# The first three tiles' attention in float32 as loaded, and the next three tiles' scores too

## The chip, the cores and the metric

The kernel runs on one core of a Trainium2 chip. The core has a matrix engine (TensorE, PE in the rows, with its weight loads as PEld), a vector engine (VectorE, DVE), an activation engine (ScalarE, ACT), a general engine (GpSimd, POOL) and a queue that issues transfers (SyncE, SP). The metric is the device time in microseconds (us) of one execution, as a median over runs. One further execution was recorded by the hardware profiler; all rows below come from it.

## The reference

The input is q, k and v of 4 batches, 8 heads, 768 positions and a head size of 64, weights of two further layers, and two integers.

```
scores = scale * q @ k.T + bias          # bias: -slope[h] * distance
scores = where(global or local, scores, -1e9)   # first 8 columns; 96 columns back
a = softmax(scores);  x = a @ v                 # x: 3072 x 512
h = x @ w_in;  x2 = (h * sigmoid(h)) @ w_out    # 512 -> 2048 -> 512
# then a soft mixture of experts: 32 slots, softmax of x2 @ phi
# over tokens and over slots, 8 small two-layer experts, and back
```

All of it is float32 in the reference; w_in and w_out arrive as float64.

## The kernel before

The 3072 rows are 24 tiles of 128. Six tiles make a batch (t is the tile's number in its batch, u its slot in a ring of four for keys and values). A tile attends to its own 128 columns and, unless t is 0, to the tile before it, whose first eight columns are overwritten with the batch's global columns (kg for keys, vg for values). Chunks of three tiles go through the two dense layers: `l1_step` makes 128 hidden columns of a chunk, `l2_part` the second layer.

Precision comes from float16 pairs. `hi` (lines 191 to 195) rounds a value to float16, `lo` (199 and 201) makes the float16 remainder, and a product is three TensorE matmuls. HE, HLO, PHE, PLE are strings that name for each tile the engine of these steps (A is ACT, V is DVE, P is POOL). `split(T)` does this for q, k and v of a tile, `s_step(T, pr)` computes the scores of two heads (line 293), the bias and maximum (298, DVE) and the exponential (299, ACT), and after each second pair splits four heads' probabilities and turns them with a transfer that transposes (314). `flip` is the other way to turn: TensorE transposes in float32 (214) into a PSUM bank, from which `hi` and `lo` read. PTE names for the first three tiles which half uses it; before, only the last of six does. `pv_step(T, half)` multiplies the turned probabilities by v (336), and for half 1 normalises (344 to 346) and makes the transposed float16 pair of the result that `l1_step` reads.

The first six tiles (`paired`) have q and k of two heads stacked on 128 partitions, so that a head's score matmul uses 64 partitions; the others have the layout of q_l and k_l. Loads go to the staging buffers stage_m, for tiles 1 and 2 to space that is used later.

`conv(p)` turns one of 16 pieces of float64 weights (1 MB each, loaded by `w_ahead` at 411 into a ring of places) into float16 pairs, with steps on DVE (421, 429, 430, 448), ACT (428, 440, 443) and POOL (426, 446). Pieces 0 to 7 are w_in and 8 to 15 w_out. GATE holds some loads back until a given half tile of probabilities is done.

`first_items` gives the order of the first three tiles. The other tiles' steps (`other_items`) are spread over the dense steps of the chunk before them: tiles 3 to 5 are done while chunk 0 goes through the dense layers. On each engine the instructions then stand in a fixed order, and an engine works through its own in that order; the transfers of the SP queue likewise.

## Time and profile before

| what | us |
|---|---|
| median of 3 runs | 766.43 |
| lowest and highest | 765.55 and 767.75 |
| the profiled execution | 765.0 |
| its span, first to last instruction | 763.2 |

The span is what the rows cover; 1.8 us of the execution lie around it. Busy time of an engine is the time in which it had an instruction under way. The rows of one engine can be read against a window of the span. [...]

### The profile page before, as it was taken

Reading aid. Unit: us, or ns where it says so; the run is one execution under the profiler, and the core shown is the slowest. Engines: PE = TensorE matmul, PEld = TensorE weight load, DVE = VectorE, ACT = ScalarE, POOL = GpSimd, SP = SyncE. Lnnn points to the kernel's source line nnn. Section 1 sums busy time; section 2 is a strip of 40 time slices with the busy share of each in tenths; the row PEclk is TensorE's granted clock in tenths of the full one; section 3 lists DMA queues with packets and bytes.
Section 4 is the critical chain, followed back from the end, with each engine's and each line's share of the span. In section 5 each row is a group of like instructions: output and inputs, shape, how many; then the busy total and the mean of one; then the engine's idle time right before and its main releaser. Section 6 shows DMA issues by size and latency. Waiting matters only on the chain.

```text
span 763.2 us, 14337 instructions
## 1 busy us (share of the span) xinstructions
PE 683.0 (89%) x5559; PEld 395.0 (52%) x5559; DVE 489.0 (64%) x1108; ACT 336.6 (44%) x855; POOL 324.7 (43%) x267
## 2 busy tenths in 40 slices
PE   2477757598999999999999999999999999998995
PEld 1244423244655565556556654665466546665375
DVE  6999999997775487548735873597266306505232
ACT  7756786553552255245423542454156305303122
POOL 4689684733455356415633673337324320101000
PEclk9978969799999999999999999999999999999997
DMA  6787645565456355733563567354532694295987
GB/s 237 194 249 205 218 87 152 191 181 120 75 125 139 83 113 137 174 75 77 132 138 74 107 137 167 56 111 109 86 43 43 150 320 178 97 357 214 391 330 223
DMA packets 162747, 120.22 MB, mean 158 GB/s; under 512 B 137456, under 2 KB 147184, under 8 KB 156656
## 3 DMA queue, kind: packets, MB, share of 16 engines
q1 hardware_dynamic: 162672, 119.23, 58.4%
q8 instruction: 45, 0.74, 0.4%
q14 instruction: 30, 0.25, 0.1%
HBM read 79.10 MB, written 6.29 MB: 112 GB/s over the span
## 4 chain that ended last, share of the span: by engine, by line
PE 67%; DVE 16%; issue 5%; POOL 4%; DMA 4%; ACT 3%; SPq 0%; ACTq 0%; DVEq 0%; POOLq 0%
PE bank L480 8%; PE bank L481 8%; PE bank L482 8%; PE bank L460 8%; PE bank L462 8%; PE bank L461 8%; PE bank L293 4%; PE bank L336 3%; DVE arena L201 2%; DMA arena<-arena 2%; DVE arena L199 2%; POOL arena L193 2%; PE bank L864 2%; DVE arena L429 2%; PE bank L902 2%
## 5 line engine op out<-in xcount | busy, mean ns | idle before, releaser
L193 POOL TENSOR_SCALAR arena<-arena 128x1024 f16<-128x1024 f32 (+5 forms) x146 | 144.4, 1002 | 237.0 <-ACT arena L299 102.5
L460 PE MATMUL bank<-rows,arena 128*128 128x384 f16 x512 | 168.4, 330 | 6.2 <-ACT arena L191 4.0
L462 PE MATMUL bank<-rows,arena 128*128 128x384 f16 x512 | 168.3, 329 | 0.8 <-DVE arena L448 0.8
L461 PE MATMUL bank<-rows,arena 128*128 128x384 f16 x512 | 168.3, 329 | 0.0
L191 ACT ACTIVATE arena<-bank 128x384 f16<-128x384 f32 (+2 forms) x165 | 81.8, 505 | 177.0 <-DVE bank L466 98.7
L199 POOL TENSOR_TENSOR arena<-arena 128x1024 f16<-128x1024 f32 (+2 forms) x69 | 131.0, 1900 | 41.3 <-ACT arena L191 37.3
L299 ACT ACTIVATE arena<-arena 128x256 f32<-128x256 f32 (+1 forms) x192 | 92.2, 482 | 98.2 <-DVE arena L298 95.3
L481 PE MATMUL bank<-arena 128*128 128x512 f16 x336 | 128.9, 384 | 2.7 <-POOL arena L446 1.9
L480 PE MATMUL bank<-arena 128*128 128x512 f16 x336 | 129.1, 384 | 1.5 <-DVE arena L201 1.5
L482 PE MATMUL bank<-arena 128*128 128x512 f16 x336 | 128.7, 383 | 0.0
L201 DVE SCALAR_TENSOR_TENSOR arena<-bank,arena 128x384 f16<-128x384 f32 (+2 forms) x142 | 81.3, 572 | 32.7 <-ACT arena L191 32.0
L293 PE MATMUL bank<-arena 128*128 128x256 f16 (+3 forms) x432 | 63.4, 288 | 41.5 <-DVE arena L298 23.9
L298 DVE CUSTOM_DVE_ANT_0 arena<-bank,arena 128x256 f32<-128x256 f32 (+1 forms) x192 | 70.5, 395 | 44.2 <-PE bank L293 42.8
L466 DVE SCALAR_TENSOR_TENSOR bank<-arena,bank 128x384 f32<-128x384 f32 x128 | 71.2, 557 | 31.0 <-ACT arena L464 29.8
L199 DVE TENSOR_TENSOR arena<-arena 128x1024 f16<-128x1024 f32 (+2 forms) x50 | 74.7, 1496 | 12.6 <-POOL arena L193 12.2
L464 ACT ACTIVATE arena<-bank 128x384 f32<-128x384 f32 x128 | 61.9, 484 | 21.1 <-PE bank L462 20.8
L293 PEld LDWEIGHTS <-arena 128*128 128x128 f16 (+1 forms) x432 | 36.3, 101 | 66.5 <-issue 38.1
L462 PEld LDWEIGHTS <-arena 128*128 128x128 f16 x512 | 50.4, 99 | 35.4 <-issue 1.6
L461 PEld LDWEIGHTS <-arena 128*128 128x128 f16 x512 | 50.4, 98 | 34.5 <-issue 7.2
L460 PEld LDWEIGHTS <-arena 128*128 128x128 f16 x512 | 50.5, 99 | 31.4 <-issue 2.9
L482 PEld LDWEIGHTS <-arena 128*128 128x128 f16 x336 | 33.1, 99 | 43.9 <-issue 5.3
L480 PEld LDWEIGHTS <-arena 128*128 128x128 f16 x336 | 33.2, 99 | 38.1 <-issue 4.8
(174 smaller groups left out, 808.8 us busy)
## 6 DMA issues: line engine op xcount, KB each, us to landing
arena<-in_w_dram SPq DMA_DIRECT2D x31, 1024.0 KB, 7.4
arena<-in_q_l_dram SPq DMA_DIRECT2D x18, 512.0 KB, 3.7
arena<-in_k_l_dram SPq DMA_DIRECT2D x18, 512.0 KB, 4.0
arena<-in_w_in_dram SPq DMA_DIRECT2D x8, 1024.0 KB, 5.7
arena<-in_w_out_dram SPq DMA_DIRECT2D x8, 1024.0 KB, 4.9
arena<-in_v_l_dram SPq DMA_DIRECT2D x24, 256.0 KB, 3.0
out_dram<-arena SPq DMA_DIRECT2D x4, 768.0 KB, 7.6
out_dram<-arena SPq DMA_DIRECT2D x8, 384.0 KB, 5.0
```

What stands on the lines that cost most here:

```text
L191: A.activation(out=out, in_=in_, func=AF.Copy, scale=p2(e))
L193: G.tensor_scalar(out=out, in0=in_, scalar1=p2(e), scalar2=0.0, op0=ALU.mult, op1=ALU.add)
L199: (V if eng == "V" else G).tensor_tensor(out=out, in0=in_, in1=h, op=ALU.subtract)
L201: V.scalar_tensor_tensor(out=out, in0=in_, scalar=p2(e), in1=h, op0=ALU.mult, op1=ALU.subtract)
L293: mm(sp[i][:, :w] if t == 0 else sp[i].rearrange("p (s c) -> p s c", s=2), qd[r, 4 * y + h], kv, start=(j == 0), stop=(j == len(terms) - 1))
L299: A.activation(out=pw, in_=pw, func=AF.Exp, scale=-1.0, bias=nmx[:, T, h:h + 1], accum_out=psum_[T % 2][:, h:h + 1])
L460: mm(hp, wh, x[:, 0, k], start=(k == 0), stop=False)
L461: mm(hp, wh, x[:, 1, k], start=False, stop=False)
L462: mm(hp, wl, x[:, 0, k], start=False, stop=(k == 3))
L480: mm(op, gh, woh[:, f, 0], start=(f == 0), stop=False)
L481: mm(op, gh, woh[:, f, 1], start=False, stop=False)
L482: mm(op, gl, woh[:, f, 0], start=False, stop=(f == 15))
```

## The change

Tiles 0 to 2 keep q, k and v as the float32 numbers that were loaded. Their scores are one float32 matmul per head (before: three of float16), their probabilities are turned on TensorE in float32 and copied by ACT to float32, and the product with v is one float32 matmul per head and block (before: three). No float16 parts of q, k or the probabilities are made for them, and of v only those of tile 2 and of the eight global rows, which tile 3 needs. Tiles 3 to 5 have float32 scores too, from q and k as loaded; their probabilities and v stay in pairs.

The float32 keys lie in the same ring as the pairs did (kr32 is a view of kr: z is now the half of a tile's columns), so a tile's keys are loaded by two transfers with runs of 64 numbers. q of these tiles goes to q16's buffers and to a part of stage_m, v to other parts of it. The global rows of v reach tile 1's buffer by a small transfer from memory, in place of a POOL copy. The load of tile 5 stands after tile 3's last score step, before it stood ahead of the third; that of tile 4 stays behind the split of tile 3. The scale of v, which the pairs carried, goes into the normalisation.

```
--- before.py
+++ after.py
@@ -89,7 +89,7 @@
 BE = 'A'
 NPAIR = 6
 HLO = 'VPVVVV'
-PTE = 'DDDDDA'
+PTE = 'A'
 XTE = 'VDA'
 GLE = 'PQPVPPVPPVPPPPVP'
 GATE = {1: (0, 0), 2: (0, 1), 3: (1, 0), 4: (1, 1), 5: (2, 0), 6: (2, 1)}
@@ -180,6 +180,14 @@
         p16 = [ar.new([2, 4, 256], F16) for _ in range(2)]
         pt0 = ar.off
         pt = [ar.new([2, 4, 2, 128], F16) for _ in range(2)]
+
+        kr32 = kr.bitcast(F32)
+        kg32 = kg.rearrange("p z h c -> p (z h c)").bitcast(F32)[:, 0:32].rearrange("p (h c) -> p h c", h=H // 2)
+        q32 = [q16[i].rearrange("p h c -> p (h c)").bitcast(F32).rearrange("p (h c) -> p h c", h=H // 2) for i in range(2)]
+        q32.append(stage_m[0][:, 0:4])
+        v32 = [stage_m[2].rearrange("p (h d) -> p h d", h=H)] + [stage_m[1][:, 4 * i:4 * i + 4].rearrange("p a c -> p (a c)").rearrange("p (h d) -> p h d", h=H) for i in range(2)]
+        v_next = stage_m[0][:, 4:8].rearrange("p a c -> p (a c)")
+        pt32 = [ar.view(pt0 + 4096 * i, [1024], F32) for i in range(2)]
         psum_ = [ar.new([H], F32) for _ in range(2)]
         rinv = [ar.new([H], F32) for _ in range(2)]
         x1f = ar.new([H, D], F32)
@@ -237,35 +245,47 @@
 
             return T < NPAIR
 
+        def q_of(T):
+            return q32[2 if T == 2 else T % 2]
+
         def load(T, bufs):
             if paired(T):
-                bufs = [bufs[0][:, 0:4], bufs[1][:, 0:4], bufs[2]]
-            for s, src in zip(bufs, (q_f, k_f, v_l) if paired(T) else (q_l, k_l, v_l)):
+                nc.sync.dma_start(out=q_of(T), in_=q_f[T])
+                for z in range(2):
+                    nc.sync.dma_start(out=kr32[:, z, 0:4, T % NR], in_=k_f[T][:, :, 64 * z:64 * z + 64])
+                nc.sync.dma_start(out=v32[T].rearrange("p h d -> p (h d)") if T < C0 else v_next, in_=v_l[T])
+                return
+            for s, src in zip(bufs, (q_l, k_l, v_l)):
                 nc.sync.dma_start(out=s, in_=src[T])
             staged[T] = bufs
 
         def split(T):
-            qs, ks, vs = staged.pop(T)
             t, u = T % TPB, T % NR
             he = HE[T] if T < len(HE) else "P"
             le = HLO[T] if T < len(HLO) else "V"
-            qd = q16[T % 2]
-            n = 4 if paired(T) else 8
             if paired(T):
-                qh, ql, qf = qd[:, 0:4], qd[:, 4:8], qs
+                v3 = v32[T] if T < C0 else v_next.rearrange("p (h d) -> p h d", h=H)
+                if T == 0:
+                    hi("P", kg32, kr32[:, 0, 0:4, u, 0:8], 0)
+                    hi("A", vg[0:8, :, 0], v3[0:8], E_V)
+                    lo("V", vg[0:8, :, 1], v3[0:8], E_V, vg[0:8, :, 0])
+                elif T >= C0 - 1:
+                    hi(he, v16[:, u, :, 0], v3, E_V)
+                    lo("V", v16[:, u, :, 1], v3, E_V, v16[:, u, :, 0])
+                if T == C0 - 1:
+                    hi("P", v16[0:8, u], vg[0:8], 0)
             else:
-                qh, ql, qf = qd, qd[64:128], qs[64:128]
-            hi(he, qh, qs, E_QK)
-            lo("P" if le == "P" else "V", ql, qf, E_QK, qh if paired(T) else ql)
-            hi(he, kr[:, 0, 0:n, u], ks, E_QK)
-            lo("V" if le == "V" else "P", kr[:, 1, 0:n, u], ks, E_QK, kr[:, 0, 0:n, u])
-            v3 = vs.rearrange("p (h d) -> p h d", h=H)
-            hi(he, v16[:, u, :, 0], v3, E_V)
-            lo("V", v16[:, u, :, 1], v3, E_V, v16[:, u, :, 0])
-            if t == 0:
-                hi("P", kg[:, :, 0:n], kr[:, :, 0:n, u, 0:8], 0)
-            if T == 0:
-                hi("P", vg[0:8], v16[0:8, u], 0)
+                qs, ks, vs = staged.pop(T)
+                qd = q16[T % 2]
+                hi(he, qd, qs, E_QK)
+                lo("P" if le == "P" else "V", qd[64:128], qs[64:128], E_QK, qd[64:128])
+                hi(he, kr[:, 0, :, u], ks, E_QK)
+                lo("V" if le == "V" else "P", kr[:, 1, :, u], ks, E_QK, kr[:, 0, :, u])
+                v3 = vs.rearrange("p (h d) -> p h d", h=H)
+                hi(he, v16[:, u, :, 0], v3, E_V)
+                lo("V", v16[:, u, :, 1], v3, E_V, v16[:, u, :, 0])
+                if t == 0:
+                    hi("P", kg, kr[:, :, :, u, 0:8], 0)
             if t == 2:
                 absmax(T // TPB, v16[:, u, 0:2, 0], AX.XY)
 
@@ -278,19 +298,27 @@
             else:
                 sp = [bS[pr % 2][:, 256 * i:256 * i + 256] for i in range(2)]
             pfb = pf[half]
-            if t == 0 and T < C0 and PTE[2 * T + half] != "D":
+            if t == 0 and T < C0:
                 pfb = pfb.rearrange("p h c -> p (h c)")[:, 0:512].rearrange("p (h c) -> p h c", h=4)
-            qd = q16[T % 2]
             for i in range(2):
-                h, r, terms = (pr, slice(64 * i, 64 * i + 64), ((0, 0), (0, 1), (1, 0))) if paired(T) else (2 * pr + i, slice(0, 128), ((0, 0), (0, 1)))
-                for j, (y, z) in enumerate(terms):
+                if paired(T):
+                    r = slice(64 * i, 64 * i + 64)
                     if t == 0:
-                        kv = kr[r, z, h, u]
+                        kv, so = kr32[r, :, pr, u], sp[i][:, :w].rearrange("p (z c) -> p z c", z=2)
+                    else:
+                        kv = (kr32[r, :, pr, u - 1:u + 1] if u > 0 else kr32[r, :, pr, 0::NR - 1]).rearrange("p z s c -> p s z c")
+                        so = sp[i].rearrange("p (s z c) -> p s z c", s=2, z=2)
+                    mm(so, q_of(T)[r, pr], kv, start=True, stop=True)
+                    continue
+                h = 2 * pr + i
+                for z in range(2):
+                    if t == 0:
+                        kv = kr[:, z, h, u]
                     elif u > 0:
-                        kv = kr[r, z, h, u - 1:u + 1]
+                        kv = kr[:, z, h, u - 1:u + 1]
                     else:
-                        kv = kr[r, z, h, 0::NR - 1]
-                    mm(sp[i][:, :w] if t == 0 else sp[i].rearrange("p (s c) -> p s c", s=2), qd[r, 4 * y + h], kv, start=(j == 0), stop=(j == len(terms) - 1))
+                        kv = kr[:, z, h, 0::NR - 1]
+                    mm(sp[i][:, :w] if t == 0 else sp[i].rearrange("p (s c) -> p s c", s=2), q16[T % 2][:, h], kv, start=(z == 0), stop=(z == 1))
             for i in range(2):
                 h = 2 * pr + i
                 bi = bias0[:, h] if t == 0 else biasw[:, h, 0:256] if u > 0 else biasw[:, h, 128:384]
@@ -298,16 +326,24 @@
                 V.tensor_tensor_reduce(out=pw, in0=sp[i][:, :w], in1=bi, scale=-p2(-2 * E_QK - 3), scalar=3e38, op0=ALU.add, op1=ALU.min, accum_out=nmx[:, T, h:h + 1])
                 A.activation(out=pw, in_=pw, func=AF.Exp, scale=-1.0, bias=nmx[:, T, h:h + 1], accum_out=psum_[T % 2][:, h:h + 1])
             if pr == 3 and 1 <= t < TPB - 1:
-                n = 4 if paired(T) else 8
-                hi("P", kr[:, :, 0:n, u, 0:8], kg[:, :, 0:n], 0)
+                if paired(T):
+                    hi("P", kr32[:, 0, 0:4, u, 0:8], kg32, 0)
+                else:
+                    hi("P", kr[:, :, :, u, 0:8], kg, 0)
             if lp == 1:
                 pb, ptb = p16[half], pt[half].rearrange("p z h s c -> p (z h s) c")
                 if t == 0:
                     pb = pb.rearrange("p z h c -> p (z h c)")[:, 0:1024].rearrange("p (z h c) -> p z h c", z=2, h=4)
-                if T < C0 and PTE[2 * T + half] != "D":
-                    n = w // 32
-                    flip(ptb[:, 0:n], ptb[:, n:2 * n], pfb.rearrange("p h c -> p (h c)"), PTE[2 * T + half])
-                    held = ptb[:, 2 * n - 1, 127:128]
+                if T < C0:
+                    p32, src = pt32[half], pfb.rearrange("p h c -> p (h c)")
+                    for i in range(0, w // 32, 4):
+                        tb = bW[flips[0] % 4]
+                        flips[0] += 1
+                        for j in range(4):
+                            tr(tb[:, 128 * j:128 * j + 128], src[:, 128 * (i + j):128 * (i + j) + 128], ident)
+                        cp = PTE[flips[0] % len(PTE)]
+                        (A.copy if cp == "A" else V.tensor_copy)(out=p32[:, 128 * i:128 * i + 512], in_=tb)
+                    held = p32[:, 4 * w - 1:4 * w]
                 else:
                     hi(PHE[T] if T < len(PHE) else CFG["phi"], pb[:, 0, :, :w], pfb[:, :, :w], 0)
                     lo(PLE[T] if T < len(PLE) else CFG["plo"], pb[:, 1, :, :w], pfb[:, :, :w], 0, pb[:, 0, :, :w])
@@ -331,17 +367,25 @@
             for hh in range(4):
                 h = 4 * half + hh
                 n = 0
+                if T < C0:
+                    nb = len(blocks)
+                    for s in range(nb):
+                        i = 128 * (nb * hh + s)
+                        mm(o[:, h], pt32[half][:, i:i + 128], v32[T - (nb - 1) + s][:, h], start=(s == 0), stop=(s == nb - 1))
+                    continue
                 for s, slot in blocks:
                     for z, y in ((0, 0), (0, 1), (1, 0)):
                         mm(o[:, h], ptb[:, z, hh, s], v16[:, slot, h, y], start=(n == 0), stop=(n == 3 * len(blocks) - 1))
                         n += 1
             if half == 1:
-                if 1 <= t < TPB - 1:
+                if 1 <= T < C0 - 1:
+                    nc.sync.dma_start(out=v32[T][0:8].rearrange("p h d -> p (h d)"), in_=v_l[0][0:8])
+                elif 1 <= t < TPB - 1 and T >= C0:
                     hi("P", v16[0:8, u], vg[0:8], 0)
                 if t == TPB - 2 and T + 2 < NTILE:
                     hi("P", vg[0:8], v16[0:8, (T + 2) % NR], 0)
                 ri = rinv[T % 2]
-                V.tensor_scalar(out=ri, in0=psum_[T % 2], scalar1=1e-9, scalar2=None, op0=ALU.add)
+                V.tensor_scalar(out=ri, in0=psum_[T % 2], scalar1=1e-9, scalar2=p2(-E_V) if T < C0 else 1.0, op0=ALU.add, op1=ALU.mult)
                 V.reciprocal(out=ri, in_=ri)
                 V.tensor_tensor(out=x1f, in0=o, in1=ri.rearrange("p (h o) -> p h o", o=1).to_broadcast([128, H, D]), op=ALU.mult)
                 xb = x16[T % 2]
@@ -383,13 +427,15 @@
                 items.append(lambda T=T: s_step(T, 1))
                 if T + 1 < NTILE:
                     items.append(lambda T=T: split(T + 1))
-                if T + 2 < NTILE:
+                if T + 2 < NTILE and not paired(T + 2):
                     items.append(lambda T=T: load(T + 2, stage_m))
                 items.append(lambda T=T: s_step(T, 2))
                 if T > C0:
                     items.append(lambda T=T: pv_step(T - 1, 1))
                     mark[T - 1] = len(items)
                 items.append(lambda T=T: s_step(T, 3))
+                if paired(T + 2):
+                    items.append(lambda T=T: load(T + 2, None))
             items.append(lambda: pv_step(NTILE - 1, 0))
             items.append(lambda: pv_step(NTILE - 1, 1))
             mark[NTILE - 1] = len(items)
@@ -706,11 +752,10 @@
         for i, src in enumerate((n_global, n_local)):
             nc.sync.dma_start(out=cw[:, 2 * i:2 * i + 2], in_=src.bitcast(I32).rearrange("(o n) -> o n", o=1).to_broadcast([128, 2]))
         nc.sync.dma_start(out=rel.rearrange("p s c -> p (s c)"), in_=shapes[:, 0:384])
-        load(0, stage_m)
+        load(0, None)
         nc.sync.dma_start(out=ident, in_=shapes[:, 384:])
         for T in range(1, C0):
-            o = g0 + 10240 * (T - 1)
-            load(T, [ar.view(o, [H, 128], F32), ar.view(o + 4096, [H, 128], F32), ar.view(o + 8192, [DM], F32)])
+            load(T, None)
             if T == 1:
                 w_ahead()
         ph = ar.view(g0 + 20480, [4, NS], F32)
```

## Rows read from the trace of the kernel before

**Rows 1.** The page: the span, and busy time of two engines.

```profile
span 763.2 us, 14337 instructions
...
PE 683.0 (89%) x5559; PEld 395.0 (52%) x5559; DVE 489.0 (64%) x1108; ACT 336.6 (44%) x855; POOL 324.7 (43%) x267
```

**Rows 2.** Busy time by window: start, end, length, each engine, clock, DMA share, GB/s.

```profile
40.00:50.00 10.00, 6.24 (x56) 2.93 (x54) 9.44 (x21) 5.56 (x15) 8.41 (x7) 0.98 1.06 254
50.00:60.00 10.00, 9.07 (x74) 5.40 (x72) 10.00 (x18) 7.30 (x16) 9.75 (x6) 0.51 0.72 246
...
8.00:57.80 49.80, 29.46 (x238) 15.81 (x238) 46.57 (x104) 35.71 (x93) 37.20 (x33) 0.92 0.83 241
57.80:178.00 120.20, 87.41 (x553) 42.26 (x553) 116.81 (x148) 75.65 (x127) 76.97 (x48) 0.87 0.61 171
...
200.00:700.00 500.00, 493.28 (x3905) 290.70 (x3901) 285.67 (x737) 198.00 (x568) 199.19 (x166) 1.00 0.53 129
```

**Rows 3.** The chain that ended last: start, length, what.

```profile
32.73 5.53 DMA arena<-arena
...
70.89 1.86 DVE arena L430
...
139.96 4.23 DVE arena L430
...
160.74 5.33 DMA arena<-in_w_out_dram
```

**Rows 4.** Groups by shape, 0 to 185 us, DVE: count, busy, mean ns, idle.

```profile
L199 DVE TENSOR_TENSOR arena<-arena 128x512 f16<-128x512 f32 x10 | 9.0, 912 | 0.1
...
L195 DVE TENSOR_SCALAR arena<-arena 128x512 f16<-128x512 f32 x3 | 3.8, 1279 | 0.0
...
L199 DVE TENSOR_TENSOR arena<-bank,arena 128x512 f16<-128x512 f32 x2 | 1.3, 674 | 0.0
```

**Rows 5.** Timeline, DVE: start, length, instruction.

```profile
14.42 0.68 DVE L201 SCALAR_TENSOR_TENSOR arena<-arena 128x512 f16<-128x512 f32 x1
...
31.45 1.21 DVE L199 TENSOR_TENSOR arena<-arena 128x1024 f16<-128x1024 f32 x1
...
36.18 1.22 DVE L199 TENSOR_TENSOR arena<-arena 128x1024 f16<-128x1024 f32 x1
...
116.94 1.22 DVE L430 SCALAR_TENSOR_TENSOR arena<-arena 128x1024 int32<-128x1024 int32 x1
```

**Rows 6.** Groups by shape, 0 to 185 us: ACT, DVE and POOL.

```profile
L428 ACT ACTIVATE arena<-arena 128x1024 uint16<-128x1024 uint8 x12 | 30.0, 2499 | 0.4 <-DMA arena<-in_w_out_dram 0.4
L430 DVE SCALAR_TENSOR_TENSOR arena<-arena 128x1024 int32<-128x1024 int32 x16 | 28.5, 1789 | 0.0
...
L199 POOL TENSOR_TENSOR arena<-arena 128x512 f16<-128x512 f32 x8 | 12.3, 1542 | 6.7 <-ACT arena L191 5.9 <-DVE arena L195 0.7
...
L191 ACT ACTIVATE arena<-bank 128x512 f16<-128x512 f32 x5 | 2.9, 593 | 6.6 <-PE bank L482 6.6
```

**Rows 7.** Groups by line and shape, 0 to 185 us: TensorE.

```profile
L293 PE MATMUL bank<-arena 64*128 64x256 f16 x120 | 19.6, 343 | 19.8 <-DVE arena L298 11.3 <-POOL arena L193 8.5
...
L336 PE MATMUL bank<-arena 128*128 128x64 f16 x264 | 12.3, 214 | 1.8 <-DMA arena<-arena 1.8
...
L214 PE MATMUL bank<-arena 128*128 128x128 f32 x16 | 4.2, 386 | 3.2 <-DVE arena L346 3.2
```

**Rows 8.** Groups of the whole span, TensorE: the float32 multiplication at line 906.

```profile
L906 PE MATMUL bank<-arena 128*128 128x128 f32 x8 | 1.4, 300 | 1.0 <-DVE arena L903 0.5 <-ACT arena L903 0.5
...
L906 PE MATMUL bank<-arena 128*128 128x256 f32 x4 | 1.1, 405 | 0.1
```

**Rows 9.** Timeline, TensorE's weight loads: line 906.

```profile
741.88 0.52 PEld L906 LDWEIGHTS bank<-arena 128*128 128x128 f32 x4 [0.79 <-DVE arena L903]
```

**Rows 10.** The page: DMA packets by size.

```profile
DMA packets 162747, 120.22 MB, mean 158 GB/s; under 512 B 137456, under 2 KB 147184, under 8 KB 156656
```

## The prediction

> **What bounds the kernel now.** I read the page first, then busy time by window, the chain of waits, groups of instructions by shape for the first 185 us, and last the timelines of single engines. The page puts TensorE at 89% of the span and VectorE at 64% [rows 1]. These are means over unlike stages. By window, from 200 to 700 us TensorE is busy 493.28 of 500.00 us at a clock of 1.00; nothing of the change lies there. Ahead of it there are two stages in which VectorE is the busier one [rows 2]. Stage one (8 to 57.8 us) is the first three tiles up to the first dense matmul: VectorE 46.57 of 49.80, TensorE 29.46, GpSimd 37.20. Stage two (57.8 to 178 us) is chunk 0 through both dense layers, with tiles 3 to 5 beside it: VectorE 116.81 of 120.20, TensorE 87.41. The chain agrees: it runs mostly through VectorE's splits and weight conversions, with a transfer that transposes at 32.73 (5.53 us) and a weight load at 160.74 among them [rows 3]. So VectorE has 163.4 us of work in 170.0 us, and what is taken off it should come off the start, as long as no other engine takes over. After 178 us everything should only be shifted.
>
> **VectorE, removed.** The float16 remainders of q and k of tiles 0, 2, 3, 4 and 5 are ten instructions, 9.0 us. Tile 1's three first parts are 3.8 us, and the remainders of tile 2's second half, which `flip` makes from PSUM, 1.3 us [rows 4]. Tile 1's remainders of the probabilities take 1.21 and 1.22 us, that of its v 0.68 us [rows 5]. Sum: 9.0 + 3.8 + 1.3 + 2.4 + 0.7 = 17.2 us. Tile 0's v remainder stays, on eight partitions; as the number of columns is the same I count no gain for it. Nothing is added to VectorE. Three of the ten remainders (one of tile 4, two of tile 5) fall into stage two: 3 x 0.9 = 2.7 us. The other 14.5 us are in stage one.
>
> **GpSimd, removed.** Tile 1's q and k remainders and tile 0's probability remainders are four of the eight GpSimd instructions at 1.54 us, 6.2 us [rows 6]; parts of tiles 2 to 4 come on top. GpSimd does not set the end of stage one, so this counts directly for nothing. It may shorten VectorE's work: step 430 of the conversions takes 1.79 us in the mean [rows 6] and 1.22 us at its shortest here [rows 5], 28.5 - 16 x 1.22 = 9.0 us over sixteen. If that excess comes from GpSimd and falls as its 114.2 us in both stages do, 6.2 / 114.2 or 5% of it is 0.5 us; four such steps per conversion make 2 us. Bounds: 0 to 2; I take 0, as which instructions meet will change. [...]
>
> **ACT.** Ten copies of 128x512 from PSUM come in; the nearest row is the evacuation at 0.593 us, so 5.9 us [rows 6]. Out go first parts of q and k of tiles 0 and 5 and of the probabilities of tiles 0, 1 and half of 2: four of 512 columns, and as many columns again and more for the probabilities, at about the same price per column at least 6 us. I count zero.
>
> **Transfers.** Five transposing transfers go (two halves of tiles 0 and 1, one of tile 2); the one on the chain took 5.53 us [rows 3]. In their place the chain has TensorE transposes and copies: eight at 0.26 plus a copy of 0.6, about 2.7 us a half. A transfer is added for each paired k (six), and one small one for v's global rows. The keys now come in runs of 256 bytes, so 1,024 per tile; 137,456 of 162,747 packets of this kernel are already under 512 bytes [rows 10], and 6,144 more are 4%. Weight data have kept the conversions waiting only 0.4 us [rows 6]. Bounds: below nothing, as the five transposes free the queue; above, a key load late by one transpose's 5.53 us at the very start, hidden as far as ACT has the bias tables to make first. I take zero. The SP queue: tile 5's load moves behind tile 3's last scores and waits there for the freeing of q's buffer. Behind it in the queue stand tile 3's and 4's transposes and weight loads; before, the same load waited for the split of tile 4, also ahead of those. I take zero, with a transfer's length as the other end.
>
> **TensorE, added.** No float32 product of this shape is in the rows. The nearest is line 906, whose four calls of 128 and two of 256 columns show as eight and four records: two records per product, 1.4 / 8 = 0.175 and 1.1 / 4 = 0.275 us each [rows 8]. Scores of tiles 1 to 5: 40 products, 80 records x 0.275 = 22.0 us, for 120 x 0.163 = 19.6 [rows 7, 8]; the low bound is the 128-column price, 14.0. So -5.6 to +2.4, two fifths of it in stage one. Tile 0 is about even. Products with v, tiles 0 to 2: 40 make 80 records, at least their weight loads (0.52 / 4 = 0.13 us [rows 9]), at most 0.175: 10.4 to 14.0 us, for 120 x 12.3 / 264 = 5.6. So +4.8 to +8.4. Transposes: 40 for 8; 32 x 4.2 / 16 = 8.4 us [rows 7], or 4.2 at the weight load's price. In stage one that is +6.8 to +17.8; I take the middle, 12, as both prices come from short groups with waits in them. TensorE's work there becomes 29.5 + 12 = 41.5 us.
>
> **The sum.** Stage one had 49.8 us for 46.6 of VectorE; now VectorE has 32.1 and TensorE 41.5, so TensorE with ACT's chain sets its end: 8 us less. The 14.5 - 8 = 6.5 us that VectorE has over are worth something only where conversions are pulled forward into the holes; the order allows some, since data are there, so half: 3.25. Stage two gives 2.7. 8 + 3.25 + 2.7 = 13.95, say 14 us. 765.0 - 14 = 751.0 us for the profiled execution; the median before is 1.4 above that execution, so 752.5.
>
> **The rivals.**
> *All of it:* VectorE stays dense with conversions, and the relief from GpSimd comes too: 17.2 + 2 = 19.2, 747 us. For it: VectorE's idle before is only 6.6 of 170 us. Against: TensorE's added work.
> *A new bound in stage one:* TensorE at the upper prices, 47.3 us, and nothing pulled forward: 2.5 + 2.7 = 5.2, 761 us. For it: TensorE's order is fixed and the transposes now stand in it, waiting for exponentials, ahead of the next scores.
> *No change:* the ring of weight places and its loads set the pace in stage two (160.74 [rows 3]), 766.4 us. Against: the 0.4 us [rows 6].
> *Slower:* TensorE at its lower clock level in stage one. The float32 work there is 11.6 (scores) + 12.2 (products) + 10.4 (40 transposes) = 34.2 us. [...] It decides from about a quarter of the work at the low level (8.3 us), where stage one gets no shorter. For it: 50 to 60 us ran at 0.51, after a pause; against: 40 to 50 us, with eight transposes, at 0.98 [rows 2]. [...]
>
> **How the numbers follow.** Chances: forecast 0.45 (748 to 757 us), all of it 0.20, a new bound 0.13, no change 0.08, slower 0.14. About 0.3%, 2.3 us, is what a measurement of this kernel can tell from no change. Faster is the sum of the first three, 0.78. The range leaves out the slower case and a little below "all of it": 745 to 767.
>
> **What would show it.** The first dense matmul (line 460), at 57.8 us, comes at about 50; TensorE's saturated stretch begins near 164 in place of 178; no float16 remainders of 512 columns for q and k ahead of tile 6; busy VectorE down by about 17 us, TensorE up by 3 to 19; the clock near 1.00 from 10 to 50 us; records of the float32 products with v between 0.13 and 0.175 us. I am wrong if the first dense matmul comes no earlier (TensorE or a key load), if it comes earlier and 178 stays (stage two's pace is not VectorE's), or if the stretch after 178 us changes its length.

## The result, and the profile after

| kernel | median, us | lowest to highest | ratio to before, 95% interval |
|---|---|---|---|
| before (5 runs beside it) | 765.55 | 765.18 to 767.75 | |
| after (5 runs) | 769.71 | 768.77 to 771.17 | 1.0051 [1.0032, 1.0069] |

The change made the kernel 0.5% slower. The forecast was 752.5 us and faster. Lines have moved in the changed kernel: float32 scores are 311, maximum 326, transposes 343 with ACT's copy 345, float32 products with v 374, normalising 388 to 390, the conversion steps 467, 474 to 476, 486, 492 and 494, remainders 207 and 209, layer one 506 to 508, layer two 526 to 528.

The page of the changed kernel, the span and busy times, against [rows 1]:

```profile
span 769.3 us, 14190 instructions
...
PE 710.8 (92%) x5503; PEld 416.1 (54%) x5503; DVE 463.7 (60%) x1090; ACT 334.9 (44%) x855; POOL 298.1 (39%) x253
```

VectorE lost 25.3 us of work, GpSimd 26.6, and TensorE gained 27.8. Busy time by window, with the columns of [rows 2]:

```profile
8.00:57.80 49.80, 48.08 (x178) 33.08 (x176) 32.09 (x77) 33.83 (x82) 15.12 (x17) 1.00 0.62 199
57.80:178.00 120.20, 92.44 (x553) 44.79 (x552) 103.61 (x155) 76.39 (x137) 72.05 (x48) 0.88 0.59 170
200.00:700.00 500.00, 492.84 (x3919) 290.23 (x3917) 287.96 (x740) 197.12 (x565) 199.44 (x164) 1.00 0.52 129
```

In stage one VectorE fell by 14.48 us. But TensorE went from 29.46 to 48.08 of 49.80: the stage has another bound. In stage two no engine is full, yet it did not get shorter: from the first dense matmul to the last layer-two matmul of chunk 0 it is 57.8 to 181.7 us before (123.9) and 60.3 to 183.7 after (123.4). The two stages do not hold quite the same work in both kernels. In TensorE's order before, the scores of all eight heads of tile 3 (24 of its 96 score records) stand ahead of the first dense matmul; in the changed kernel none does, and stage two has them. The 500 us behind it are unchanged. The last layer-one matmul of the kernel begins at 665.4, before at 662.3.

TensorE's groups in stage one (8 to 58 us) of the changed kernel, with the columns of [rows 7]:

```profile
L374 PE MATMUL bank<-arena 128*128 128x64 f32 x80 | 18.0, 417 | 0.0
L311 PE MATMUL bank<-arena 64*128 64x256 f32 x32 | 13.7, 712 | 0.4 <-DVE arena L326 0.3
L343 PE MATMUL bank<-arena 128*128 128x128 f32 x40 | 12.5, 440 | 0.1
L311 PE MATMUL bank<-arena 64*128 64x128 f32 x16 | 3.8, 496 | 8.7 <-DMA arena<-in_k_f_dram 7.5 <-DVE arena L326 1.2
```

Nearly no idle time stands before the first three: the engine works through a queue that is always ready. Two parts of its timeline say at which level (start, length, instruction):

```profile
50.33 6.93 PE L374 MATMUL bank<-arena 128*128 128x64 f32 x32
...
60.77 1.23 PE L311 MATMUL bank<-arena 64*128 64x256 f32 x4
...
64.15 0.52 PE L508 MATMUL bank<-rows,arena 128*128 128x384 f16 x1
64.47 0.46 PE L506 MATMUL bank<-rows,arena 128*128 128x384 f16 x1
...
64.92 0.33 PE L508 MATMUL bank<-rows,arena 128*128 128x384 f16 x1
65.08 0.33 PE L506 MATMUL bank<-rows,arena 128*128 128x384 f16 x1
...
67.12 0.70 PE L311 MATMUL bank<-arena 64*128 64x256 f32 x4
```

The same four score records took 1.23 us at 60.77 and 0.70 at 67.12, and dense matmuls follow each other at 0.32 us until 64.5 and at 0.16 from 64.9. So TensorE came out of stage one at the lower of two levels, although the clock column of that window says 1.00. The column reads 1.00 at both (60 to 64.5 and 64.9 to 67 us), and in the first experiment, which starts at the upper level, 0.54 for the same 8 to 57.8 us.

### The profile page after: what moved, and what is told of

It is laid out like the page before. It is cut to its first block, busy times and chain, and to the rows that moved or that the text cites. A ratio compares the mean times of both kernels' runs of the same rounds, so it can differ in the third digit from the quotient of the medians.

```text
span 769.3 us, 14190 instructions
## 1 busy us (share of the span) xinstructions
PE 710.8 (92%) x5503; PEld 416.1 (54%) x5503; DVE 463.7 (60%) x1090; ACT 334.9 (44%) x855; POOL 298.1 (39%) x253
## 4 chain that ended last, share of the span: by engine, by line
PE 75%; DVE 8%; POOL 5%; issue 5%; ACT 4%; DMA 3%; SPq 0%; POOLq 0%; ACTq 0%; DVEq 0%
PE bank L506 8%; PE bank L507 8%; PE bank L508 8%; PE bank L526 8%; PE bank L527 8%; PE bank L528 8%; PE bank L321 3%; PE bank L378 3%; PE bank L311 3%; DMA arena<-arena 2%; PE bank L909 2%; PE bank L374 2%; POOL arena L201 2%; PE bank L947 2%; POOL arena L207 2%
## 5 line engine op out<-in xcount | busy, mean ns | idle before, releaser
L201 POOL TENSOR_SCALAR arena<-arena 128x1024 f16<-128x1024 f32 (+5 forms) x137 | 131.2, 969 | 244.5 <-ACT arena L327 103.9
L207 POOL TENSOR_TENSOR arena<-arena 128x1024 f16<-128x1024 f32 (+2 forms) x64 | 121.8, 1906 | 39.0 <-ACT arena L199 34.8
L508 PEld LDWEIGHTS <-arena 128*128 128x128 f16 x512 | 50.5, 99 | 33.9 <-issue 1.4
L506 PEld LDWEIGHTS <-arena 128*128 128x128 f16 x512 | 50.5, 99 | 33.3 <-issue 6.2
L507 PEld LDWEIGHTS <-arena 128*128 128x128 f16 x512 | 50.5, 99 | 29.6 <-issue 2.5
L207 DVE TENSOR_TENSOR arena<-arena 128x1024 f16<-128x1024 f32 (+1 forms) x38 | 56.0, 1477 | 13.7 <-POOL arena L201 13.3
L528 PEld LDWEIGHTS <-arena 128*128 128x128 f16 x336 | 33.1, 98 | 40.3 <-issue 1.1
L526 PEld LDWEIGHTS <-arena 128*128 128x128 f16 x336 | 33.0, 98 | 38.5 <-issue 5.0
L527 PEld LDWEIGHTS <-arena 128*128 128x128 f16 x336 | 33.0, 98 | 34.3 <-issue 0.6
L311 PE MATMUL bank<-arena 64*128 64x256 f32 (+1 forms) x96 | 29.4, 581 | 23.8 <-DVE arena L326 11.0
```

The lines of the kernel that those rows point to most:

```text
L201: G.tensor_scalar(out=out, in0=in_, scalar1=p2(e), scalar2=0.0, op0=ALU.mult, op1=ALU.add)
L207: (V if eng == "V" else G).tensor_tensor(out=out, in0=in_, in1=h, op=ALU.subtract)
L506: mm(hp, wh, x[:, 0, k], start=(k == 0), stop=False)
L507: mm(hp, wh, x[:, 1, k], start=False, stop=False)
L508: mm(hp, wl, x[:, 0, k], start=False, stop=(k == 3))
L526: mm(op, gh, woh[:, f, 0], start=(f == 0), stop=False)
```

## The experiments

Theory A: float32 work at the lower level makes TensorE the bound of stage one. Theory B: the loss is elsewhere in the change (scores, key loads, order). Theory C: stage two is paced by links between engines, so that VectorE's freed time is worth nothing there. Times of before beside them lay between 766.6 and 767.3, beside the result at 765.55, so runs are best compared by their ratios. The first dense matmul marks the end of stage one only roughly: how many of tile 3's eight heads have their scores ahead of it differs from kernel to kernel (none in the changed kernel, five in the second experiment), and a head's two records take 0.35 us at the upper level and 0.61 at the lower (0.70 and 1.23 for four, above).

**A start at the upper level** (18 float16 matmuls in the first 7 us, ahead of the first scores):

```
+for i in range(18):
+    mm(bW[3], ones16, warm, start=True, stop=True)   # 128 x 512, constants
```

> The changed kernel with 18 float16 matmuls of 512 columns on constants in the first 7 us, in which TensorE has nothing to do; nothing else differs. In the changed kernel two heads' float32 scores (four records of 256 columns) take 1.22 us in stage one and 0.70 us at 67 us, after float16 matmuls have run. Theory A (TensorE's float32 work at the lower clock level sets stage one): if float32 work keeps the level that the float16 matmuls bring, the four records take about 0.70 us from the start, the first dense matmul comes near 40 us in place of 60.3, and the time is about 752 us; if it does not keep it, the first groups are fast and the rest at 1.22 us again, and the time is 767 to 770 us. Theory B (the chain exponential, transpose, copy, product in TensorE's fixed order sets stage one, not TensorE's speed): 769.7 us within 1.5 either way.

769.4 us, 1.0050 [1.0033, 1.0066], no better. Its windows and timeline:

```profile
8.00:57.80 49.80, 47.28 (x177) 32.43 (x175) 32.45 (x78) 34.14 (x82) 15.29 (x18) 0.54 0.63 202
```

```profile
10.87 0.69 PE L311 MATMUL bank<-arena 64*128 64x128 f32 x4 [0.29 <-DVE arena L326]
...
15.22 1.22 PE L311 MATMUL bank<-arena 64*128 64x256 f32 x2
16.38 0.90 PE L343 MATMUL bank<-arena 128*128 128x128 f32 x3
```

The small score groups run at 0.69 us (1.00 without the start), but from about 12 to 15 us on all is as in the changed kernel: the float32 work did not hold the level.

**Two float16 matmuls of 512 columns ahead of each of the ten groups of transposes**, on top of that:

```
 tb = bW[flips[0] % 4]
 ...
+for j in range(2):
+    mm(tb, ones16, warm, start=True, stop=True)
 for j in range(4):
     tr(tb[:, 128 * j:128 * j + 128], ...)
```

> As e1_preheat, and two further float16 matmuls of 512 columns on constants ahead of each of the ten groups of probability transposes, so 20 in stage one. Theory A: if float16 work among the float32 work holds the higher level, the scores take 0.70 us for four records throughout, the first dense matmul comes near 45 us, and the time is about 755 us; if it does not, the 20 cost 20 x 0.43 = 8.6 us in stage one and the time is about 778 us. Theory B: up to 4 us later than the changed kernel, as part of the matmuls fall into waits: 770 to 774 us.

766.89 us, 1.0012 [0.9983, 1.0041]. The level was held in parts (8 to 20 and 30 to 44 us). The first dense matmul came later, at 62.4 (five heads of tile 3 ahead of it), and still chunk 0 ended 3 us earlier, at 180.7. The ratio's interval overlaps the changed kernel's.

**Scores alone in float32** (probabilities and v in pairs as before):

```
-PTE = 'A'
+PTE = 'DDDDDA'
-    if T < C0:
-        ...
-        mm(o[:, h], pt32[half][:, i:i + 128], v32[T - (nb - 1) + s][:, h], ...)
+    for z, y in ((0, 0), (0, 1), (1, 0)):
+        mm(o[:, h], ptb[:, z, hh, s], v16[:, slot, h, y], ...)
```

> One part of the change alone: float32 scores for the first six tiles, from q and k as loaded; the probabilities and v of all tiles in float16 pairs, turned by transfers, as before the change. Theory A: TensorE loses 18.0 us of float32 products less 5.6 of float16 ones, and 32 of the 40 transposes at 0.3 us, so about 22 us of its 48 in stage one; the first dense matmul comes at 50 to 54 us, and the time is 759 to 763 us, faster than both. Theory B: the transposes' place in TensorE's order is gone too, so the same direction, but the five transposing transfers of 5 us return to the chain: 764 to 767 us.

768.39 us, 1.0013 [0.9997, 1.003]: a miss. TensorE had 31.0 of 49.8 us, and the first dense matmul came at 60.9 all the same, with no head of tile 3 ahead of it.

**Probabilities and v alone in float32** (scores of all tiles in pairs as before):

```
-mm(so, q_of(T)[r, pr], kv, start=True, stop=True)
+for j, (y, z) in enumerate(((0, 0), (0, 1), (1, 0))):
+    mm(sp[i][:, :w], qd[r, 4 * y + h], kr[r, z, h, u], ...)
```

> The kernel before with one part of the change: the probabilities of tiles 0 to 2 are turned and multiplied by v in float32; all scores stay in float16 pairs. Beside the run with the scores alone (768.4) it splits the change. If TensorE at its lower clock level is what the change pays in stage one (first theory), nearly all of it is here: scores alone left TensorE at 31.0 of 49.8 us, the whole change at 48.1, so this one should show about 46 to 47, the first dense matmul at 59 to 61, and 766 to 771. If the loss comes from the float32 scores or the new order of the key loads (second theory), it comes out at the time of before or below, 760 to 766, with TensorE well under 45. If the order of VectorE's conversion steps sets the end of stage one whatever the attention costs (third theory), the first dense matmul stays within 57 to 62 and the time within 765 to 769.

768.73 us, 1.0043 [1.0018, 1.0069]; first dense matmul at 61.2, with all eight heads ahead of it, as before. TensorE was at 40.5, not 46 to 47: with float16 scores between them, the float32 records ran at the upper level from 28 to 45 us (eight product records in 1.11 us at 28.61, 1.97 at 18.39). Each half of the change alone thus has room on TensorE and ends stage one no earlier. A can't be all of it.

**Weight conversions ahead of their turn** in the changed kernel (`START = [3, 8, 13, 18, 21, 99, 99, 99]`, four more emitted between the tiles' steps):

> The changed kernel with the conversions of weight pieces 1 to 4 put after the 8th, 13th, 18th and 21st item of the first three tiles, in place of beside the dense steps; nothing is added. It is for the step of the prediction that half of VectorE's free time in stage one is used. Theory A: TensorE sets stage one, so the first dense matmul stays at 60 us within 2, VectorE is busier in stage one than 32 of 49.8 us, and if VectorE's conversions pace stage two, that stage is 3 to 7 us shorter: 763 to 767 us. Rival C (stage two's pace is a chain over ACT, VectorE, GpSimd and the loads, in which VectorE's spare time is worth nothing): 769.7 us within 1.5.

777.26 us, 1.0139 [1.0116, 1.0162]: first dense matmul at 66.5, chunk 0 done at 192. Both expectations missed. Conversion steps put among the tiles' steps delay the tiles (tile 2's last product with v ends at 62.7, in the changed kernel at 57.3) and are not paid back.

**Less work for VectorE** (step 467, a range check, left out for the eight pieces of w_out, about 7.6 us), in the changed kernel and in the one before:

```
+if p < 8:
     V.tensor_scalar(out=odd16.bitcast(U16), in0=u16[:, :, 3], scalar1=0x7000, ...)
```

> The changed kernel without VectorE's range check of weight pieces 8 to 15 (one instruction of 0.95 us in the mean for each piece; the matmul that sums the check up runs on the last piece's data, so that TensorE's work is the same). It takes 7.6 us off VectorE in stage two and nothing off another engine; the range check of w_out is what it leaves out. If VectorE's work paces stage two (the forecast's reading): 4 to 7 us faster than the changed kernel, 763 to 766 us. Rival C (stage two runs along a chain over all engines in their fixed orders, VectorE's spare time is worth nothing): within 1.5 us of the changed kernel, 768 to 771 us.

> The same removal in the kernel before, whose VectorE was busy 116.8 of 120.2 us in stage two. The range check of w_out is left out. Forecast's reading: 5 to 7.6 us faster than before, 758 to 761 us. Rival C: within 1.5 us of before, 765 to 768 us.

768.77 us, 1.0018 [1.0003, 1.0033], and 766.0, 0.9994 [0.9983, 1.0004]. By the ratios that is some 2.5 us for the changed kernel (0.9 by the medians), between the two expectations, and at most 1.3 us for the one before. In the kernel before, whose VectorE was busy for 97% of stage two, its work there fell from 116.81 [rows 2] to 111.05 us (54.11 up to 113 us, 56.94 behind). Chunk 0 did end earlier for it, at 178.5 (before 181.7), and in the changed kernel at 177.0 (183.7). Part of that is one link: the matmul that sums the check up waits for the last step 467, 4.37 us in the changed kernel and 2.02 in the one before. And most of it is lost at once, as TensorE then waits for a transposing transfer (4.17 us in the changed kernel without the check). The first line is the changed kernel's, the second is of the run without the check:

```profile
177.59 1.01 PE L469 MATMUL bank<-arena 128*1 128x512 bf16 x2 [4.37 <-DVE arena L467]
```

```profile
182.50 0.50 PE L551 MATMUL bank<-arena 128*128 128x32 f16 x12 [4.17 <-DMA arena<-arena]
```

At the end of chunk 1's second layer 1.3 us of the 3.2 are left, and 1.5 of the 6.7. So 5.8 us less for a VectorE at 97% bought 1.3 us at most: its busy time alone did not pace the stage.

**The splits of the probabilities of tiles 3 to 5 off GpSimd** (to ACT and VectorE), in both kernels:

```
-PHE = 'AAPPAP'   PLE = 'PVPPPV'
+PHE = 'AAPAAA'   PLE = 'PVPVVV'
```

> The changed kernel with the probability splits of tiles 3 to 5 taken off GpSimd: the first parts of tiles 3 and 5 go to ACT, the remainders of tiles 3 and 4 to VectorE, four letters in the two strings that name the engines. VectorE gets about four instructions of 1.2 to 3 us, GpSimd loses eight of 1.3 to 3 us. Rival C, with GpSimd's splits as the slow link (TensorE waits 3.68 us on one, and GpSimd has 29.9 us of the chain in stage two against 19.7 before): stage two 4 to 8 us shorter, 762 to 766 us. Forecast's reading (VectorE paces): 3 to 5 us slower, 773 to 775 us. If neither: within 1.5 us of 769.7.

> The same four letters in the kernel before. Forecast's reading: VectorE, busy 97% of stage two, gets 5 to 10 us more, and the kernel is 4 to 8 us slower, 770 to 774 us. Rival C: 0 to 4 us faster than before, 762 to 766 us.

766.17 us, 0.9987 [0.9971, 1.0003], in the changed kernel; 770.19, 1.0049 [1.0032, 1.0066], in the one before. The same edit gains 3.5 us after the change (4.9 by the ratios) and costs about as much before it. The trace of the changed kernel shows what there was to gain. First VectorE's, then GpSimd's, then the transfer queue's timeline:

```profile
111.40 1.70 DVE L476 SCALAR_TENSOR_TENSOR arena<-arena 128x1024 int32<-128x1024 int32 x1
...
135.66 1.57 DVE L475 TENSOR_SCALAR arena<-arena 128x1024 uint16<-128x1024 uint16 x1 [2.81 <-ACT arena L474]
137.27 1.23 DVE L476 SCALAR_TENSOR_TENSOR arena<-arena 128x1024 int32<-128x1024 int32 x1
```

```profile
117.75 3.22 POOL L207 TENSOR_TENSOR arena<-arena 128x1024 f16<-128x1024 f32 x1 [1.12 <-DVE arena L207]
```

```profile
121.00 2.44 SPq L350 DMA_TRANSPOSE arena<-arena  x1
124.51 0.34 SPq L457 DMA_DIRECT2D arena<-in_w_out_dram  x1
...
160.78 0.52 SPq L457 DMA_DIRECT2D arena<-in_w_out_dram  x1
```

Step 476 at 111.40 is the eleventh of sixteen; the kernel before made its eleventh at 133.6, so the conversions were 22 us ahead. The twelfth came at 137.27, against 139.96 [rows 3]. Between them the next piece's load goes out at 124.51 (before at 123.79). Two things hold it there. In the transfer queue it stands behind a transposing transfer, which starts at 121.00 when GpSimd's remainder of the probabilities ends (117.75 + 3.22). And its place in the ring is free only after range check 467 on VectorE (123.45 to 124.48): this is the ninth such step, that of the piece that had the place, while step 476 is already at the eleventh piece. Without the check (the run above) the load still waited for a transposing transfer at 120.68 and went out at 123.60, hardly earlier, though its last load went out at 155.20. The waits of the transfer queue in the changed kernel's stage two (who waited for whom: us, times, longest):

```profile
SPq L350 <- POOL arena L207: 24.8, 4, 9.8
SPq L457 <- DVE arena L467: 20.7, 6, 6.8
```

The last load is issued at 160.78, before at 160.74 [rows 3]: the lead is lost in the queue. With the splits moved, the waits of line 350 for GpSimd fall to 6.7 us and those of the loads for step 467 to 9.8, the last load goes out at 153.76, and chunk 0 ends at 178.2.

What the edit costs in the kernel before does not show in stage two, where VectorE had 118.62 of 120.2 us: its last load goes out at 154.68 and chunk 0 ends at 180.8, 0.9 us earlier. It is 1.7 us late at the end of chunk 1's second layer (258.5 for 256.8), and about 2 more are lost between 400 and 490 us, where the granted clock reads 0.98 from 400 to 500 in place of 1.00. Why is open.

**Also the remainders of four weight pieces off GpSimd** (on top of the moved splits):

```
-LOE = 'PVVPVVPVVPPVVVVV'
+LOE = 'PVVVVVVVVVVVVVVV'
```

> The changed kernel with the splits of tiles 3 to 5 off GpSimd (766.2 alone) and also the remainders of four weight pieces (3, 6, 9 and 10) made by VectorE in one step in place of a scaling on ACT and a subtraction on GpSimd. GpSimd loses four steps of about 2.5 us, VectorE gains four of about 1.2. If slow links through GpSimd pace stage two while VectorE has room (theory), another 1 to 3 us go: 763 to 765.5. If VectorE is what it waits for, it gets slower, 767 to 770; if neither, 766.

771.92 us, 1.0054 [1.0037, 1.007], slower than without this second edit. Not every step on GpSimd is a slow link; with these four on VectorE its work from 113 to 178 us is 63.02 of 65, as in the kernel before.

**Both helpful edits together** (float16 matmuls ahead of the transposes, and the splits moved):

> The changed kernel with both edits that helped alone: float16 matmuls ahead of each group of transposes (766.9 alone, 2.8 under the changed kernel of that call), and the splits of the probabilities of tiles 3 to 5 off GpSimd (766.2 alone, 3.5 under). If the two act in different stages and both are on the chain, they add: 769.7 - 2.8 - 3.5 = 763.4, so 762 to 765 and faster than before. If either only moves work to the place where the other one waits, 765.5 to 767.

762.33 us, 0.9933 [0.9919, 0.9947]: they add, and this version beats both kernels. The last load is at 155.85 and chunk 0 ends at 176.5. Its first dense matmul comes at 64.9 (five heads of tile 3 ahead), later than in either kernel: the float16 matmuls' gain is not an earlier end of stage one, and where it comes from was not traced.

**TensorE at the upper level throughout:** as the last, with two such matmuls ahead of every score step and product with v too.

```
+for j in range(2):
+    mm(bW[flips[0] % 4], ones16, warm, start=True, stop=True)
```

> As the last, with two more float16 matmuls of 512 columns ahead of every score step and every product with v of tiles 0 to 2, so that TensorE should stay at its upper level through stage one. First theory alone: the float32 work then costs half, TensorE waits, and the first dense matmul comes at 50 to 54; 757 to 761. If VectorE's order (conversion steps ahead of tile 2's last steps) is the next thing that ends stage one, the first dense matmul stays at 57 to 62 although the records of the float32 products are short (four score records in 0.70 us, not 1.22), and the time stays at 762 to 767.

764.56 us, 0.9958 [0.9945, 0.9971]. TensorE's groups from 8 to 58 us, and a stretch of the chain of waits:

```profile
L315 PE MATMUL bank<-arena 64*128 64x256 f32 x44 | 12.5, 428 | 1.7 <-DVE arena L330 1.6
L383 PE MATMUL bank<-arena 128*128 128x64 f32 x80 | 9.8, 272 | 0.0
L349 PE MATMUL bank<-arena 128*128 128x128 f32 x40 | 8.5, 290 | 2.5 <-ACT arena L331 2.5
```

```profile
16.75 2.42 ACT arena L483
...
19.19 1.33 DVE arena L484
...
20.54 1.24 DVE arena L485
...
24.63 2.15 POOL arena L501
...
28.67 2.50 POOL arena L481
...
36.38 2.49 POOL arena L481
```

The products take 9.8 us in place of 18.0, the transposes 8.5 in place of 12.5. Yet the first dense matmul comes at 57.5 (six heads ahead): the chain now runs through conversion steps (481 to 501 here) that stand among the tiles' steps. Nor does an early end of stage one carry through by itself: it is 7.4 us earlier than in the last run, but chunk 0 ends only 1.7 earlier (174.8) and the kernel 2.2 later.

**Conversions kept out of stage one.** First the loads of pieces 1 to 6 were to be held back to later half tiles (in the last kernel, the changed one and the one before). I quote the first expectation:

> The run with float16 matmuls ahead of every step (764.6; TensorE at its upper level, first dense matmul at 57.5), with the loads of weight pieces 1 to 6 held back to the last halves of the first three tiles, so that no conversion step but those of piece 0 can stand ahead of a tile's steps. If conversion steps ahead of the tiles' steps end stage one there (third theory), the first dense matmul comes at 47 to 53 and VectorE's work from 8 to 57.8 us falls from 38.7 to about 30. What that is worth: if stage two then only makes up the conversions, chunk 0 ends where it did (about 175 us) and the time is 763 to 767; if stage two keeps its length, 757 to 761. If stage one is a chain of the attention itself, the first dense matmul stays at 56 to 59.

763.52, 777.03 and 773.15 us, with the first dense matmul at 54.4, 74.6 and 57.4. For the question they settle nothing: two of the loads had no gate of their own, came at 15.7 us, and VectorE's work in the first of them was 38.56 us, where it had been 38.72. In the second, expected at 50 to 59, conversion steps that came late still stood ahead: the chain runs through 474, 475, 476, 467, 475 and 494 from 56.17 to 72.16. So each load got its gate, behind the last half of tile 2:

```
-GATE = {1: (0, 0), 2: (0, 1), 3: (1, 0), 4: (1, 1), 5: (2, 0), 6: (2, 1)}
+GATE = {1: (2, 1), 2: (2, 1), 3: (2, 1), 4: (2, 1), 5: (2, 1), 6: (2, 1)}
-p = nload[0]
-if p < 16 and GATE.get(p) == (T, half) and holder.get(place[p]) is None:
+for p in range(16):
+    if GATE.get(p) == (T, half) and holder.get(place[p]) is None:
         G.tensor_scalar(out=ar.view(place[p], [16], F32)[:, 0:1], in0=held, ...)
```

> As the run with float16 matmuls ahead of every step (764.6, first dense matmul at 57.5), but each of the weight pieces 1 to 6 is loaded only after the last half tile of the first three; in the run with the loads held back before (763.5, first dense matmul at 54.4) two pieces still came at 15.7 us and VectorE had as much conversion work in stage one as without. Now no conversion step but those of piece 0 can be there. If conversion steps ahead of the tiles' steps are the bound behind TensorE (third theory), VectorE's work from 8 to 57.8 us falls and the first dense matmul comes at 46 to 51. If the chain of the attention itself is, it stays at 53 to 58. The time says little here: stage two has all the conversions before it, so 770 to 785 in either case.

> The changed kernel with the same six loads after the last half tile. No conversion step but those of piece 0 is in stage one; what is left there is the attention with its float32 work at the lower level. First theory (TensorE's added work at the lower level is the first bound of the changed kernel): the first dense matmul comes no earlier than 55, against 60.3. If conversion steps are the first bound in the changed kernel: 46 to 52. The time is 775 to 790 either way.

> The kernel before with the same six loads after the last half tile. If VectorE's total work ended stage one before the change (the prediction's reading), taking some 12 us of conversion steps off it brings the first dense matmul from 57.8 to 46 to 50. If it was a chain through several engines that the conversions only filled up, it stays at 54 to 58. 775 to 790 either way.

| kernel | first dense matmul | with no conversions but piece 0 | VectorE, 8 to 57.8 | time, us |
|---|---|---|---|---|
| before | 57.8 | 53.0 | 41.35 | 778.81 |
| after | 60.3 | 61.4 | 19.27 | 787.13 |
| after, TensorE at the upper level | 57.5 | 51.6 | 24.70 | 785.53 |

In the order of the right column 8, 5 and 4 heads of tile 3 stand ahead of that matmul (left: 8, 0 and 6), so 61.4 holds some 3 us of scores that 60.3 does not; on the other hand five matmuls of the check, some 2.5 us, are missing from it. The changed kernel's stage one with 19.27 us left for VectorE ends hardly earlier, if at all, and its chain of waits is TensorE's alone from 28.78 to 46.61 and again from 47.08 on:

```profile
44.78 0.62 PE bank L343 x2
45.40 1.21 PE bank L311 x4
46.61 0.42 DVE arena L326 x2
...
47.08 1.22 PE bank L311 x2
48.29 0.62 PE bank L343 x2
...
52.28 5.87 PE bank L373 x28
58.14 1.16 PE bank L311 x4
59.30 1.04 PE bank L222 x4
60.34 1.16 PE bank L311 x4
61.50 0.75 PE bank L505 x2
```

So A holds for the kernel as changed: TensorE's added work at the lower level is enough to end its stage one there. Kept at the upper level, it gains 5.9 us from the missing conversions (51.6, just outside both expected ranges and nearer to the first), and the kernel before 4.8 us (53.0, between its two ranges): there conversion steps stand in the way.

The conversion steps are not far behind in the changed kernel either. In three executions that have its stage one (the check left out, the splits moved, the four remainders moved too) TensorE rose to its upper level at 47 to 50 us. The last products with v ended at 53.5 to 53.9 in place of 57.3, and still the first dense matmul came at 59.3 to 59.9, behind ACT's conversion steps. With the splits moved, from TensorE's timeline and the chain of waits:

```profile
49.84 3.68 PE L374 MATMUL bank<-arena 128*128 128x64 f32 x32
...
59.89 0.48 PE L506 MATMUL bank<-rows,arena 128*128 128x384 f16 x1 [0.97 <-ACT rows L199]
```

```profile
55.91 2.53 ACT arena L474
```

So two bounds lie within about 1 us of each other, and only the run that took both away (51.6) ended stage one much earlier.

## Why the prediction was wrong

**VectorE, removed.** That stage one lost 14.48 us, for 14.5 forecast, is luck. The first parts and remainders (lines 195, 199 and 201) lost 18.6 us there (21.6 to 3.0), and 3.1 us of score maxima (line 298) went to stage two with tile 3; against that the conversion steps grew by 4.5 (14.4 to 18.9), and some of these steps overlap. Tile 0's v remainder, counted for no gain, takes 0.68 us on its eight partitions (at 9.29 in the changed kernel), as the one on 128 at 23.42 does. Stage two lost 13.2 us, not 2.7. Its conversion steps fell from 75.7 to 62.4 us: one 475 and one 476 fewer, and the others shorter. The groups of the changed kernel up to 185 us:

```profile
L476 DVE SCALAR_TENSOR_TENSOR arena<-arena 128x1024 int32<-128x1024 int32 x16 | 26.7, 1670 | 0.2
L475 DVE TENSOR_SCALAR arena<-arena 128x1024 uint16<-128x1024 uint16 x16 | 24.1, 1506 | 11.5 <-ACT arena L474 8.6 <-POOL arena L472 2.7
L494 DVE SCALAR_TENSOR_TENSOR arena<-arena 128x1024 f16<-128x1024 f32 x11 | 15.3, 1393 | 0.1
```

Step 476 had 1,789 ns [rows 6], 475 had 1,678 and 494 had 1,744 before. The three together lost 8.0 us. GpSimd's relief, set to 0 with a bound of 2, was mis-sized, though in stage two GpSimd itself lost only 4.9 us (76.97 to 72.05). It bought no time.

**TensorE, added.** This step failed first. 6.8 to 17.8 us were expected in stage one; 18.6 came, and that without tile 3's scores, which the window holds before. The float16 scores of the kernel before, from 8 to 58 us:

```profile
L293 PE MATMUL bank<-arena 64*128 64x256 f16 x72 | 13.7, 381 | 9.8 <-DVE arena L298 9.0 <-POOL arena L193 0.8
...
L293 PE MATMUL bank<-arena 64*128 64x128 f16 x24 | 3.3, 291 | 12.6 <-ACT arena L191 8.2 <-DVE arena L298 3.6 <-DVE arena L199 0.8
```

48 of the 72 are of tiles 1 and 2, so tiles 0 to 2 took about 13.7 x 48 / 72 + 3.3 = 12.4 us, and 17.5 in float32 (the groups above): 5 us more, where the prediction had -2.2 to +1.0. The products take 18.0 / 80 = 0.225 us a record, not 0.13 to 0.175, and the transposes 0.31, not 0.26. The prices of [rows 8, 9] come from a stretch at a granted clock of 1.00 (733 to 750.6 us); at the upper level the products show 9.8 / 80 = 0.12 and the transposes 8.5 / 40 = 0.21 us.

**The clock.** The 0.98 of [rows 2], from 40 to 50 us, was used to set the slower rival aside. Lengths tell more. TensorE's timeline of the kernel before has six float16 score records at either level:

```profile
28.51 0.83 PE L293 MATMUL bank<-arena 64*128 64x256 f16 x6 [0.75 <-POOL arena L193]
...
76.02 0.51 PE L293 MATMUL bank<-arena 64*128 64x256 f16 x6
```

Its stage one, too, ran at the lower level there, and could afford it with 29.46 us of work. It rose only about 42 us (two float32 transposes took 0.69 us at 40.47 and 0.45 at 42.76), so the 0.98 was right for the rest of its ten microseconds alone. With only float16 matmuls added, at the start and ahead of the groups of transposes, the level was held in parts (8 to 20 and 30 to 44 us in the second experiment). Whether the transposes or the other float32 matmuls brought it down was not shown: no run separates them.

**The sum of stage one.** It took the larger of two engines' work: 41.5, 8 us less. With 48.1 us on TensorE it became 2.5 us more. Nor would a TensorE at 41.5 us have given the 8 us: where it came up early without an edit to stage one, or stayed up throughout, conversion steps ended the stage at 57.5 to 59.9, which the sum of two engines' work does not contain. The slower rival's mechanism is thus the right one for the stage as it ran. That it would decide from about a quarter of the float32 work took that level for half the speed, the author's estimate; the runs showed 0.225 us for 0.12 a product record, 0.31 for 0.21 a transpose and 1.23 for 0.70 four score records, so 1.5 to 1.8 times the length, and the first dense matmul 2.5 us later.

**Conversions pulled forward, 3.25 us.** They were pulled forward, by 22 us at the eleventh. The step counted that as a gain. It was none, since the weight loads wait in the transfer queue and for places in the ring, which the prediction had put at zero. In stage one they stand among the tiles' steps and cost 5 to 6 us where TensorE does not bind.

**Stage two, 2.7 us.** It failed with VectorE 13.2 us lighter; in the kernel before 5.8 us less were worth 1.3 at most. Busy time of 97% was not the bound by itself: the steps largely fill the time that the links (split, transposing transfer, weight load, conversion, check) leave. The "no change" rival named the ring of weight loads and was set aside on a wait of 0.4 us at ACT [rows 6]; the wait stands in the transfer queue (24.8 and 20.7 us above), where no compute engine's idle time shows it. That reading rests on one move of splits in the changed kernel; no run changed the queue's order alone, and in the kernel before the same move brought the last load 6 us forward and made the kernel slower.

**After 178 us.** The shift carries through (+3.1 us at 665 us). The profiled execution, the slowest of its five, loses 3 us more behind that; I have not traced these.

What stays open: how stage two's links share the loss among themselves (the splits' move helped; four other steps' move did not), why the float16 matmuls helped although stage one ended later with them, and what a lead at the end of chunk 0 loses behind it.

## What to carry to other kernels

Before pricing float32 work on TensorE, find the same record at two places of the trace and compare lengths: here the clock column read 1.00 with four score records at 1.23 us and at 0.70. An engine that is 97% busy is the bound only if taking work off it shortens the kernel; one run with a step left out tells that, read at the end of the stage and at the end of the kernel. Before an early or late first matmul is taken for the length of a stage, count what stands ahead of it in the engine's order. When work comes off an engine, try giving it some of another engine's: the same moved splits gained some 3.5 us after the change and cost as much before it.

## What the runs showed of the hardware

- In the first experiment TensorE, 95% busy (47.28 of 49.80 us) with float32 scores, transposes and products, fell from the upper to the lower level by about 15 us (two score records took 1.22 us at 15.22) and stayed there (a granted clock of 0.54 in the mean of the window). In three other executions the same float32 work began at the lower level and rose at 47 to 50 us (with the splits moved, 32 product records at 49.84 took 3.68 us). With two float16 matmuls of 512 columns ahead of each step it stayed up: 32 product records at 51.30 us took 3.79 us, where the changed kernel's took 6.93.
- One float32 product of 64 columns shows as two records of 0.225 us at the lower level and 0.12 us at the upper.
- VectorE's conversion steps were 7 to 20% shorter in the changed kernel, where GpSimd had 26.6 of its 324.7 us less (476: 1,789 to 1,670 ns, 475: 1,678 to 1,506, 494: 1,744 to 1,393). In the kernel before the five steps 430 with no GpSimd work beside them took 1.17 to 1.24 us, the other eleven 1.52 to 4.23. Why steps 475, 476 and 494 differ in this was not shown.
